# Gated linear attention and top-1 experts on one core: swapped values loaded on their own, masks tied to scalings, the floor inside the scan, copies without gaps

## The chip, the cores and the metric

One core of one Trainium2 chip runs the whole program. The metric is the device time of one execution in microseconds. The kernel before took 412.81 us in the median of three runs (411.1, 412.81 and 415.93).

## The reference

Two stages. The first is an attention without softmax, with a state that decays by channel: B=4, H=8, S=768, D=48, all in fp32, and alpha between 0.8 and 1:

```python
for t in range(S):
    state = alpha[:, :, t, :, None] * state + np.einsum('bhd,bhe->bhde', k[:, :, t], v[:, :, t])
    y[:, :, t] = np.einsum('bhd,bhde->bhe', q[:, :, t], state)
```

The second takes the 3072 rows of 384 (all heads of a token), adds a bias by modality to the logits of eight experts, takes the highest, and computes `gate * (relu(x @ w1[e]) @ w2[e])` with 1024 hidden channels for that expert alone.

## The kernel before

**Tiling of the attention.** 24 units of 128 tokens (`NU`), six to a sequence (`NC`), each with all eight heads as four pairs (`NP`); a head's 48 channels lie in 64 partitions or columns, with a gap of 16. Within a unit the recurrence is solved with scans and matmuls:

- `load` (L148): alpha, k and q of a unit go into one of four sets of buffers (`nat_a0` to `nat_a3`, likewise k and q), v into one of six (`vt0` to `vt5`). Tokens are partitions, and each token brings eight runs of 192 bytes. All are issued on SP's queue.
- `turn_decay` (L247): PE turns alpha, ACT copies it to X (L249).
- `decay`: a scan on DVE from the right gives G, the products of decays up to the unit's end (L258); its floor `amin` by a `tensor_scalar` (L262); a reciprocal of that (L263); a second scan from the left gives Fw (L264).
- `scale_k`, `scale_q`: PE turns k and q, DVE multiplies by G (kh, L280) and Fw (qh, L286).
- `scores`: PE multiplies kh with qh (L301); ACT copies the result to scT in two pieces (L302, L306); POOL clears what lies above the diagonal in two halves with `affine_select` (L305), then copies the values of four heads from one half of the partitions to the other, vt to vs (L309), since half of the products need them there.
- `keys`: PE turns kh back (L317), ACT copies it to knat (L319).
- `combine`: U is the state times the unit's whole decay (L335, DVE); y and the state's update are accumulated by small matmuls (L342); S, the new state, is an addition on DVE.
- `outputs`, `rows`, `logits_turned`, `logits`: ACT copies y to yt (L397); PE turns it (L404), ACT copies it to xs (L409), and SP stores it (L410); the router's logits come from yt by matmuls (L416), in one step out of two for two units.
- `guard` (L268): one ACT instruction that accumulates relu of alpha's bits less a bound over the unit. Its sum tells, after the loop, whether any alpha lay out of range, in which case a slow path computes the attention again.

**Staging.** A step `s` of the loop (L845) works on several units at once: it loads ahead, turns the decays of unit `s`, scales k and q of `s-1`, makes scores and keys of `s-2`, combines `s-3`, and puts out `s-4`. After the loop the expert stage runs, for the most part matmuls.

**What sets the order.** A scheduler places each instruction in its engine's queue from the data's dependences and its own model of times. Every engine works through its own queue in order, and SP's queue issues the loads and stores in order. `issue_after(name)` holds an instruction behind the one marked with that name; `pin` keeps PE's instructions of the loop in program order from the fifth step on. So the queues of ACT, DVE, POOL and SP may come out in another order when an instruction is added or moved elsewhere.

Of the kernel before, what the change touches and what calls it, by code (L numbers as in the profile page):

```python
# [8 lines left out]
F32 = mybir.dt.float32  # L9
# [5 lines left out]
ALU = mybir.AluOpType  # L15
# [6 lines left out]
P = 128  # L22
B, H, S, D = 4, 8, 768, 48
# [31 lines left out]
def attention_moe(ctx: ExitStack, tc: tile.TileContext, q, k, v, alpha, mid, wg, mb, w1, w2, out):  # L55
# [29 lines left out]
    for i in range(NB):  # L85
        for n, val in (("a", 1.0), ("k", 0.0), ("q", 0.0)):
            t = ac.tile([P, H, 64], F32, name=f"nat_{n}{i}")
            nat[n, i] = t
            pool.memset(t[:, :, D:], val)

    VT = []
    for i in range(NV):
        t = ac.tile([P, H, 64], F32, name=f"vt{i}")
        VT.append(t)
        pool.memset(t[:, :, D:], 0.0)
    VS = []
    for i in range(2):
        t = ac.tile([P, NP, 64], F32, name=f"vs{i}")
        VS.append(t)
        pool.memset(t[:, :, D:], 0.0)  # L100
# [12 lines left out]
    def issue_after(name):  # L113
        return tc.issue_after(mark[name].ins) if name else nullcontext()
# [28 lines left out]
    def load(i, names="akqv"):  # L143
        b, c = divmod(i, NC)
        for n, t in (("a", alpha), ("k", k), ("q", q), ("v", v)):
            if n in names:
                src = t[b, :, c * P : (c + 1) * P, :].rearrange("h t d -> t h d")
                sp.dma_start((VT[i % NV] if n == "v" else nat[n, i % NB])[:, :, :D], src)  # L148

    wgs = cp.tile([P, ND, E], F32, name="wgs")  # L150
    sp.dma_start(wgs, wg.rearrange("(c p) e -> p c e", p=P))
# [15 lines left out]


    DR = ac.tile([P, NP * SEG + 1], F32, name="DR")
    vec.memset(DR, 0.0)  # L170
    vec.memset(DR[:, SEG :: SEG], 1.0)
    X, DF, UB = [], [], []
    for i in range(2):
# [64 lines left out]
    def seg(t, lo):  # L238
        return t.rearrange("p (a b) -> p a b", b=SEG)[:, :, lo : lo + P]
# [13 lines left out]
    def decay(i):  # L253
        x, d = X[i % 2], DF[i % 2]
        Fw = sb.tile([P, NP * SEG], F32, name="Fw", bufs=3)
        G = sb.tile([P, NP * SEG + 1], F32, name="G", bufs=4)
        with issue_after("kh" if i else None):
            vec.tensor_tensor_scan(  # L258
                G[:, 1:][:, ::-1], x[:, 1:][:, ::-1], DR[:, 1:][:, ::-1], 0.0, op0=ALU.mult, op1=ALU.add
            )  # L260
        ac1 = amin[:, i]
        vec.tensor_scalar(ac1, G[:, 1::SEG], AFLOOR, None, op0=ALU.max)  # L262
        vec.reciprocal(d[:, 0::SEG], ac1)  # L263
        vec.tensor_tensor_scan(Fw, x[:, :-1], d, 0.0, op0=ALU.mult, op1=ALU.add)  # L264
        st[i, "G"], st[i, "F"] = G, Fw

# [16 lines left out]
    def scale_q(i):  # L283
        qh = sb.tile([P, NP, P], F32, name="qh", bufs=3)
        pq = trans(i, "q")
        vec.tensor_tensor(qh, pq, seg(st[i, "F"], 1), op=ALU.mult)  # L286
        st[i, "q"] = qh

    def scores(i):

        kh, qh = st[i, "k"], st[i, "q"]
        s = sb.tile([P, 12, 64], F32, name="scT")
        pp = banks.rearrange("p g (x t) -> p g x t", t=64)
        for z in range(2):
            for o in range(2):
                for a in range(2):
                    for g in range(2):
                        j, r = 2 * a + o, slice(64 * g, 64 * g + D)
                        x = slice(j, j + 1) if z else slice(j, 4 + o + 1, 4 - 2 * a)
                        t = halves[1] if z else slice(0, P)  # L300
                        pin(pe.matmul(pp[halves[z ^ a], g, x], kh[r, j, halves[z]], qh[r, j, t], start=True, stop=True))  # L301
        act.copy(s[:, :8].rearrange("p (g x) t -> p g x t", g=2), pp[:, :, :4])  # L302
        for b in range(2):
            m = s[halves[b], :8]
            pool.affine_select(m, m, [[0, 8], [1, 64]], ALU.is_ge, 0.0, base=0, channel_multiplier=-1)  # L305
        mark["sc"] = act.copy(s[:, 8:].rearrange("p (g x) t -> p g x t", g=2), pp[:, :, 4:6])  # L306
        st[i, "s"] = s
        for b in range(2):
            mark["vs"] = pool.tensor_copy(VS[i % 2][halves[b], :, :D], VT[i % NV][halves[1 - b], H // 2 :, :D])  # L309

    def keys(i):

        kh = st[i, "k"]
        if i % NC < NC - 1:
            p = ps.tile([P, NP, P], F32, name="tr", bufs=3)
            for j in range(NP):
                pin(pe.transpose(p[:, j], kh[:, j], ident))  # L317
            kn = sb.tile([P, NP, P], F32, name="knat")
            act.copy(kn, p)  # L319
            st[i, "n"] = kn  # L320

    def chain(ins, other, kind):
        info = mybir.DependencyInfo(kind, mybir.DependencyReason.DATA)
        tc.add_manual_dep(ins.ins, other.ins.name, info, reason="row tiles")
        return ins

    def combine(i):

        c = i % NC
        qh, vt, vs, sc = st[i, "q"], VT[i % NV], VS[i % 2], st[i, "s"]  # L330
        U = UB[i % 2]
        if c > 0:
            S0 = st[i, "S"]
            A = st[i, "G"][:, 1::SEG].unsqueeze(2).broadcast_to([P, NP, D])
            vec.tensor_tensor(U[:, :, :D], S0, A, op=ALU.mult)  # L335

        yk = ps.tile([P, 2, 512], F32, name="y")
        fresh = {(b, x) for b in range(2) for x in range(2)}
# [2 lines left out]
        def part(b, x, lo, hi, *operands, stop=False):  # L341
            ins = pin(pe.matmul(yk[halves[x], b, lo:hi], *operands, start=(b, x) in fresh, stop=stop))  # L342
            fresh.discard((b, x))
            if done:
                chain(ins, done[-1], mybir.DependencyClass.NoSync)
            if gate:
                chain(ins, gate.pop(), mybir.DependencyClass.Sync)
            done.append(ins)

        def phase(n):  # L350
            if n:
                gate.append(chain((pool if i < NU - 3 else act).nop(), done[-1], mybir.DependencyClass.Sync))
            if c > 0 and n == 0:
                for a in range(2):
                    for o in range(2):
                        for g in range(2):
                            j = 2 * a + o
                            part(g, o, P * a, P * (a + 1), U[halves[g], j], qh[halves[g], j])
            if c < NC - 1:
                kn = st[i, "n"]  # L360
                for a in range(2):
                    for o in range(2):
                        for g in range(2):
                            j, r, lo = 2 * a + o, halves[o ^ n], 2 * P + D * a
                            part(o, g, lo, lo + D, kn[r, j, halves[g]], vt[r, 2 * j + g, :D])
            for a in range(2):
                for g in (a, 1 - a):
                    for o in range(2):
                        r, z = halves[g ^ n], g ^ n ^ a
                        h = 4 * a + 2 * o + g  # L370
                        xs = (4 * g + 2 * a + o, 8 + 2 * g + o)
                        cuts = ((0,), (1,)) if n and z == 0 and c == 0 else ((0, 1),) if z == 0 else ((0,),)
                        for cut in cuts:
                            x = slice(xs[cut[0]], xs[cut[-1]] + 1, xs[1] - xs[0])
                            lo = P * a + 64 * (z or cut[0])
                            last = n == 1 and a == 1 and cut == cuts[-1]
                            part(g, o, lo, lo + 64 * len(cut), vs[r, h - H // 2] if a else vt[r, h], sc[r, x], stop=last)
# [21 lines left out]

    def rows(i):  # L400

        p = ps.tile([P, NP, P], F32, name="tr", bufs=3)
        for j in range(NP):
            pin(pe.transpose(p[:, j], st[i, "y"][:, j], ident))  # L404
        xs = sb.tile([P, DM], F32, name="xs", bufs=4)
        xv = xs.rearrange("p (a o g d) -> p g a o d", a=2, o=2, g=2)
        pv = p.rearrange("p (g a) (o e) -> p g a o e", g=2, o=2)
        for g in range(2):
            act.copy(xv[:, g], pv[:, g, :, :, :D])  # L409
        sp.dma_start(xd[row(i) : row(i) + P, :], xs)  # L410

    def logits_turned(i):
# [407 lines left out]

    def early(e):
        early_places(e)
        with issue_after("vs"):
            gather(e, row(EARLY[e]))

    def early_gates():
        with issue_after("vs"):
            for e in range(NA):
                gather_gates(e, row(EARLY[e]))

# [14 lines left out]
    for s in range(NU + 3):  # L845
# [4 lines left out]
            turn_decay(s)  # L850
        if 0 <= s - 4:
            outputs(s - 4)
        if s == NU + 1:
            first_inputs()
        if 0 <= s - 1 < NU:
            scale_k(s - 1)
        if 0 <= s - 1 < NU:
            scale_q(s - 1)
        if s < NU:
            decay(s)  # L860
        if s > 4 and s % 2 == 0 and s <= NU:
            logits(s - 5)
        if s > 4 and s % 2:
            logits_turned(s - 4)
        if 0 <= s - 4:
            rows(s - 4)
        if 0 <= s - 2 < NU:
            keys(s - 2)
        steps = combine(s - 3) if 0 <= s - 3 < NU else iter(())
        if s == NU + 2:  # L870
            first_layer(0, 0, own=True)
# [3 lines left out]
        if s == NU + 2:  # L875
            first_layer(0, 1)
        next(steps, None)
        if s < NU:
            guard(s)
        if s == 5:  # L880
# [250 lines left out]
```

## Time and profile before

| | |
|---|---|
| median of the runs | 412.81 us (411.1 to 415.93) |
| profiled execution | 411.67 us, span 409.9 us, clock 0.976 |
| PE busy over the span | 365.8 us (89%) |
| DVE busy | 278.2 us (68%) |
| ACT busy | 214.7 us (52%) |
| POOL busy | 159.2 us (39%) |

The span holds the attention loop with its start-up in the first 172 us or so, and the expert stage behind it. The shares over the whole span hide that the two have different limits, so windows of the timeline are read for the loop: 16 to 40 us (start-up), 40 to 130 us (even steps) and 130 to 172 us (the loop's end). A step of the loop is told by PE's turning of alpha (`tr<-ident,nat_a`, L244): the seventh begins at 39.52 us, the twenty-second at 129.40 us. In a row of the timeline stand the start, the duration, the engine, the line, the operation and its tiles, how many instructions the row holds, and in brackets the idle time before it with what ended it. In a row of a group stand the busy time, the mean of one in ns, and the idle time before with its releasers.

### The profile page before, as it was taken

To read this page: it belongs to the slowest core of one execution; us is meant where nothing else is said; L and a number is where in the kernel's file an instruction comes from. 1 tells how busy PE (TensorE), PEld (TensorE's weight loads), DVE (VectorE), ACT (ScalarE), POOL (GpSimd) and SP (SyncE) were. 2 spreads that over 40 slices of the span, in tenths; PEclk is the share of its full clock that TensorE was granted. 3 is DMA by queue.
4 is the path that set the end of the run, shared out by engine and by line. 5 is a ranking of instruction groups with operands and counts; after the bars stand their busy time and mean duration, and the time that the engine had idled before them with its cause. 6 is when DMAs were issued, how large, how long until landed. Compare 5 with 4: busy or idle time off the path is not lost. (4 is left out here: it accounts for less than half of the span.)

```text
span 409.9 us, 11915 instructions
## 1 busy us (share of the span) xinstructions
PE 365.8 (89%) x4779; PEld 340.4 (83%) x4779; DVE 278.2 (68%) x550; ACT 214.7 (52%) x425; POOL 159.2 (39%) x224
## 2 busy tenths in 40 slices
PE   4867878898989878998997999999999999999993
PEld 3656768777768766778996999999999999999993
DVE  6984978997999993579659394745838465472420
ACT  3445466556566434445458384664837547473430
POOL 8603553454454353501747324233432523221010
PEclk9996999999999988999998999999999999999998
DMA  7999777868876176803998756929656683730000
GB/s 137 189 188 226 167 168 168 163 146 176 169 160 154 42 248 231 297 22 118 387 380 292 267 173 218 302 86 340 219 205 207 208 302 104 295 100 19 21 25 25
DMA packets 132664, 75.26 MB, mean 184 GB/s; under 512 B 103777, under 2 KB 120222, under 8 KB 132600
## 3 DMA queue, kind: packets, MB, share of 16 engines
q1 hardware_dynamic: 128504, 64.57, 56.2%
q0 software_dynamic: 4096, 9.85, 7.0%
q8 instruction: 39, 0.64, 0.6%
q14 instruction: 25, 0.20, 0.1%
HBM read 64.95 MB, written 9.65 MB: 182 GB/s over the span
## 5 line engine op out<-in xcount | busy, mean ns | idle before, releaser
L976 PE MATMUL tr<-xL,w1H 128*128 128x256 f32 x264 | 74.8, 288 | 0.0
L977 PE MATMUL tr<-xH,w1L 128*128 128x256 f32 x264 | 74.0, 285 | 0.0
L975 PE MATMUL tr<-xH,w1H 128*128 128x256 f32 x264 | 72.5, 286 | 1.7 <-DVE hL L982 1.7
L998 PE MATMUL sc<-w2H,hH 128*128 128x384 f32 x192 | 65.8, 343 | 2.3 <-ACT hH L979 1.3
L305 POOL TENSOR_SCALAR_AFFINE_SELECT scT<-scT 64x512 f32<-64x512 f32 x48 | 34.3, 715 | 79.2 <-ACT scT L302 67.2
L999 PE MATMUL sc<-w2L,hH 128*128 128x384 f32 x192 | 64.5, 336 | 0.0
L1000 PE MATMUL sc<-w2H,hL 128*128 128x384 f32 x192 | 64.4, 336 | 0.0
L949 DVE TENSOR_TENSOR w2L<-w2r,w2H 128x768 fp32r<-128x768 f32 x52 | 49.2, 957 | 20.2 <-ACT w2H L947 18.3
L916 POOL DMA_INDIRECT out_dram<-os,odx x25 | 26.7, 1068 | 89.7 <-ACT os L1002 60.9
L949 DVE TENSOR_TENSOR w1L<-w1r,w1H 128x768 fp32r<-128x768 f32 x44 | 41.5, 955 | 22.1 <-ACT w1H L947 22.1
L975 PEld LDWEIGHTS tr<-xH,w1H 128*128 128x128 f32 x264 | 49.9, 193 | 2.1 <-issue 1.9
L947 ACT CAST w2H<-w2r 128x768 fp32r<-128x768 f32 x52 | 42.4, 835 | 16.6 <-PE sc L1000 16.6
L976 PEld LDWEIGHTS tr<-xL,w1H 128*128 128x128 f32 x264 | 51.1, 193 | 0.0
L977 PEld LDWEIGHTS tr<-xH,w1L 128*128 128x128 f32 x264 | 51.0, 193 | 0.0
L725 POOL DMA_INDIRECT xg<-xd,idx x26 | 27.9, 1073 | 55.1 <-PE y L937 46.5
L947 ACT CAST w1H<-w1r 128x768 fp32r<-128x768 f32 x44 | 36.0, 835 | 15.9 <-PE tr L976 15.1
L998 PEld LDWEIGHTS sc<-w2H,hH 128*128 128x128 f32 x192 | 36.1, 188 | 4.3 <-ACT hH L979 1.5
L982 DVE SCALAR_TENSOR_TENSOR hL<-tr,hH 128x512 fp32r<-128x512 f32 x46 | 31.3, 683 | 11.0 <-ACT hH L979 11.0
L268 ACT ACTIVATE junk<-nat_a,bhi 128x384 f32<-128x384 uint32 x24 | 14.8, 617 | 42.8 <-DMA nat_a<-in_alpha_dram 42.7
L258 DVE TENSOR_TENSOR_SCAN G<-X,DR 128x516 f32<-128x516 f32 x24 | 33.3, 1388 | 5.4 <-ACT X L249 5.0
L999 PEld LDWEIGHTS sc<-w2L,hH 128*128 128x128 f32 x192 | 36.2, 188 | 0.0
L1000 PEld LDWEIGHTS sc<-w2H,hL 128*128 128x128 f32 x192 | 36.1, 188 | 0.0
(220 smaller groups left out, 756.7 us busy)
## 6 DMA issues: line engine op xcount, KB each, us to landing
w1r<-in_moe_w_dram SPq DMA_DIRECT2D x26, 768.0 KB, 7.2
w2r<-in_moe_w_dram SPq DMA_DIRECT2D x26, 768.0 KB, 7.5
nat_a<-in_alpha_dram SPq DMA_DIRECT2D x24, 192.0 KB, 3.6
nat_k<-in_k_dram SPq DMA_DIRECT2D x24, 192.0 KB, 3.4
nat_q<-in_q_dram SPq DMA_DIRECT2D x24, 192.0 KB, 3.5
vt<-in_v_dram SPq DMA_DIRECT2D x24, 192.0 KB, 3.5
xd<-xs SPq DMA_DIRECT2D x24, 192.0 KB, 2.9
xg<-xd,idx POOLq DMA_INDIRECT x26, 3.9
```

The source lines that it names most:

```text
L258: vec.tensor_tensor_scan(G[:, 1:][:, ::-1], x[:, 1:][:, ::-1], DR[:, 1:][:, ::-1], 0.0, op0=ALU.mult, op1=ALU.add)
L305: pool.affine_select(m, m, [[0, 8], [1, 64]], ALU.is_ge, 0.0, base=0, channel_multiplier=-1)
L725: pool.indirect_dma_start(xg[i % NX][:, u], None, xd[0:rows], ix, bounds_check=rows - 1, oob_is_err=False)
L947: act.copy(hi, src)
L949: vec.tensor_tensor(lw, src, hi.bitcast(F32), op=ALU.subtract)
L975: pe.matmul(hp[:, z], wH[:, d, fs], xH[:, d], start=(d == 0), stop=False)
L976: pe.matmul(hp[:, z], wH[:, d, fs], xL[:, d], start=False, stop=False)
L977: pe.matmul(hp[:, z], wL[:, d, fs], xH[:, d], start=False, stop=(d == ND - 1))
L982: mark[f"h{j}L"] = vec.scalar_tensor_tensor(hL, hp, 0.0, hH.bitcast(F32), op0=ALU.max, op1=ALU.subtract)
L998: pe.matmul(op, hH[:, z, us], wH[:, z], start=(f == 0), stop=False)
L999: pe.matmul(op, hH[:, z, us], wL[:, z], start=False, stop=False)
L1000: pe.matmul(op, hL[:, z, us], wH[:, z], start=False, stop=(f == NF - 1))
```

## The change

1. **Swapped values.** `vs` is no longer copied by POOL. Behind each load of v, two loads of half the partitions and half the heads bring the other half's values from HBM; `vs` has six buffers instead of two.
2. **Masks.** POOL's two `affine_select` of a unit move one step later, to a function of their own; the first is tied behind U (DVE), the second behind kh (DVE). U is computed earlier in the step, in `state`. The gathers of the expert stage that were held behind the vs copies are now held behind a mask.
3. **Floor.** The scan of G takes the maximum with the floor at each element (`max` with DR in place of adding DR), so the reciprocal reads G. ACT copies the last column of G to `amin`, once a unit; the scan is held behind qh instead of kh.
4. **Copies.** `knat` and `xs` are copied without the gaps of 16, xs in one instruction instead of two, knat into two buffers of its own. `keys` stands ahead of `rows` in the step.

```diff
@@ load
                 sp.dma_start((VT[i % NV] if n == "v" else nat[n, i % NB])[:, :, :D], src)
+                for z in range(2 if n == "v" else 0):
+                    sp.dma_start(VS[i % NV][halves[1 - z], :, :D], src[halves[z], H // 2 :])
@@ set-up
-    vec.memset(DR, 0.0)
+    vec.memset(DR, AFLOOR)
@@ decay
-        with issue_after("kh" if i else None):
+        with issue_after("qh" if i else None):
             vec.tensor_tensor_scan(
-                G[:, 1:][:, ::-1], x[:, 1:][:, ::-1], DR[:, 1:][:, ::-1], 0.0, op0=ALU.mult, op1=ALU.add
+                G[:, 1:][:, ::-1], x[:, 1:][:, ::-1], DR[:, 1:][:, ::-1], 0.0, op0=ALU.mult, op1=ALU.max
             )
-        ac1 = amin[:, i]
-        vec.tensor_scalar(ac1, G[:, 1::SEG], AFLOOR, None, op0=ALU.max)
-        vec.reciprocal(d[:, 0::SEG], ac1)
+        vec.reciprocal(d[:, 0::SEG], G[:, 1::SEG])
@@ scores
-        for b in range(2):
-            m = s[halves[b], :8]
-            pool.affine_select(m, m, [[0, 8], [1, 64]], ALU.is_ge, 0.0, base=0, channel_multiplier=-1)
...
-        for b in range(2):
-            mark["vs"] = pool.tensor_copy(VS[i % 2][halves[b], :, :D], VT[i % NV][halves[1 - b], H // 2 :, :D])
@@ keys
-            act.copy(kn, p)
+            kn = KN[i % 2]
+            act.copy(kn[:, :, :, :D], p[:, :, :, :D])
@@ new functions
+    def state(i):
+        if i % NC:
+            A = st[i, "G"][:, 1::SEG].unsqueeze(2).broadcast_to([P, NP, D])
+            mark["U"] = vec.tensor_tensor(UB[i % 2][:, :, :D], st[i, "S"], A, op=ALU.mult)
+
+    def mask(i):
+        s = st[i, "s"]
+        for b, behind in enumerate(("U", "kh")):
+            m = s[halves[b], :8]
+            ins = pool.affine_select(m, m, [[0, 8], [1, 64]], ALU.is_ge, 0.0, base=0, channel_multiplier=-1)
+            if behind in mark:
+                chain(ins, mark[behind], mybir.DependencyClass.Sync)
+            mark["mask"] = ins
@@ rows
-        for g in range(2):
-            act.copy(xv[:, g], pv[:, g, :, :, :D])
+        act.copy(xs.rearrange("p (x g d) -> p g x d", x=4, g=2), p.rearrange("p (g a) o d -> p g (a o) d", g=2)[:, :, :, :D])
@@ the loop
             turn_decay(s)
         if 0 <= s - 4:
             outputs(s - 4)
+        if 0 <= s - 3 < NU:
+            state(s - 3)
...
             scale_q(s - 1)
+        if 0 <= s - 3 < NU:
+            mask(s - 3)
         if s < NU:
             decay(s)
...
+        if 0 <= s - 2 < NU:
+            keys(s - 2)
         if 0 <= s - 4:
             rows(s - 4)
-        if 0 <= s - 2 < NU:
-            keys(s - 2)
...
+        if 0 < s <= NU:
+            act.copy(amin[:, s - 1], st[s - 1, "G"][:, 1::SEG])
         if s < NU:
             guard(s)
```

The scheduler's queues move with it. First SP's queue around the load of alpha for unit 13 (`nat_a1`, with k and q in `nat_k0` and `nat_q0`, and v of a unit ahead in `vt5`), between two stores of xs. Before:

```order
L410 DMA xd_60<-xs_1011 128x384
L148 DMA vt5_111<-in_v_dram 128x8x48
L148 DMA nat_a1_83<-in_alpha_dram 128x8x48
L148 DMA nat_k0_79<-in_k_dram 128x8x48
L148 DMA nat_q0_81<-in_q_dram 128x8x48
L410 DMA xd_60<-xs_1116 128x384
```

and now:

```order
L417 DMA xd_60<-xs_1029 128x384
L153 DMA vt5_115<-in_v_dram 128x8x48
L155 DMA vs5_127<-in_v_dram 64x4x48 x2
L153 DMA nat_k0_79<-in_k_dram 128x8x48
L153 DMA nat_q0_81<-in_q_dram 128x8x48
L153 DMA nat_a1_83<-in_alpha_dram 128x8x48
L417 DMA xd_60<-xs_1131 128x384
```

The two vs loads stand behind vt, and alpha has moved from second to last. It stands so for units 13, 14, 19, 21 and 23, and between k and q for unit 20; for the others alpha is still ahead of k and q, behind vs.

Next ACT's queue in the same step (`nat_a1` in `guard`; `scT` is the next scores). Before:

```order
L397 COPY yt_980<-y_1023 128x512
L268 ACTIVATE junk_171,gacc_169<-nat_a1_83,bhi_167 128x384
L418 COPY lts_1109<-rt_1104 128x256
L409 COPY xs_1116<-tr_1111 128x4x48 x2
L319 COPY knat_1125<-tr_1120 128x512
L302 COPY scT_1144<-sc_71 128x512
```

and now:

```order
L407 COPY yt_990<-y_1032 128x512
L425 COPY lts_1118<-rt_1113 128x256
L319 COPY knat1_103<-tr_1120 128x8x48
L890 COPY amin_188<-G_1109 128x4
L416 COPY xs_1131<-tr_1126 128x2x4x48
L273 ACTIVATE junk_189,gacc_187<-nat_a1_83,bhi_185 128x384
L307 COPY scT_1151<-sc_71 128x512
```

`guard` has moved from behind yt to just ahead of scT, and the copy of amin is new.

Last, ACT's queue in the start-up, around the X of unit 5 (`X1`), with the guards of units 6, 7 and 8 (`nat_a2`, `nat_a3`, `nat_a0`). Before:

```order
L268 ACTIVATE junk_171,gacc_169<-nat_a2_89,bhi_167 128x384
L302 COPY scT_547<-sc_71 128x512
L306 COPY scT_547<-sc_71 128x256
L268 ACTIVATE junk_171,gacc_169<-nat_a3_95,bhi_167 128x384
L249 COPY X1_161<-tr_596 128x4x128
L397 COPY yt_483<-y_522 128x512
L418 COPY lts_628<-rt_623 128x256
L268 ACTIVATE junk_171,gacc_169<-nat_a0_77,bhi_167 128x384
```

and now:

```order
L273 ACTIVATE junk_189,gacc_187<-nat_a2_89,bhi_185 128x384
L307 COPY scT_563<-sc_71 128x512
L308 COPY scT_563<-sc_71 128x256
L273 ACTIVATE junk_189,gacc_187<-nat_a3_95,bhi_185 128x384
L273 ACTIVATE junk_189,gacc_187<-nat_a0_77,bhi_185 128x384
L256 COPY X1_179<-tr_611 128x4x128
L407 COPY yt_500<-y_538 128x512
```

The guard of unit 8 now stands ahead of X and yt; before, it came behind both.

More of the change, by code (lines that the diff above doesn't have):

```diff
@@ L89, in attention_moe @@
             pool.memset(t[:, :, D:], val)
+    KN = []
+    for i in range(2):
+        t = ac.tile([P, NP, 2, 64], F32, name=f"knat{i}")
+        KN.append(t)
+        pool.memset(t[:, :, :, D:], 0.0)
     VT = []
@@ L96, in attention_moe @@
     VS = []
-    for i in range(2):
+    for i in range(NV):
         t = ac.tile([P, NP, 64], F32, name=f"vs{i}")
@@ L285, in scale_q @@
         pq = trans(i, "q")
-        vec.tensor_tensor(qh, pq, seg(st[i, "F"], 1), op=ALU.mult)
+        mark["qh"] = vec.tensor_tensor(qh, pq, seg(st[i, "F"], 1), op=ALU.mult)
         st[i, "q"] = qh
@@ L314, in keys @@
         if i % NC < NC - 1:
-            p = ps.tile([P, NP, P], F32, name="tr", bufs=3)
+            p = ps.tile([P, NP, 2, 64], F32, name="tr", bufs=3)
             for j in range(NP):
                 pin(pe.transpose(p[:, j], kh[:, j], ident))
-            kn = sb.tile([P, NP, P], F32, name="knat")
-            act.copy(kn, p)
+            kn = KN[i % 2]
+            act.copy(kn[:, :, :, :D], p[:, :, :, :D])
             st[i, "n"] = kn
@@ L325, in chain @@
         return ins
+    def state(i):
[10 more added lines that the diff above has]
+            mark["mask"] = ins
     def combine(i):
         c = i % NC
-        qh, vt, vs, sc = st[i, "q"], VT[i % NV], VS[i % 2], st[i, "s"]
+        qh, vt, vs, sc = st[i, "q"], VT[i % NV], VS[i % NV], st[i, "s"]
         U = UB[i % 2]
[L332 to L335, printed above, removed]
         yk = ps.tile([P, 2, 512], F32, name="y")
@@ L364, in phase @@
                             j, r, lo = 2 * a + o, halves[o ^ n], 2 * P + D * a
-                            part(o, g, lo, lo + D, kn[r, j, halves[g]], vt[r, 2 * j + g, :D])
+                            part(o, g, lo, lo + D, kn[r, j, g], vt[r, 2 * j + g, :D])
             for a in range(2):
@@ L400, in rows @@
     def rows(i):
-        p = ps.tile([P, NP, P], F32, name="tr", bufs=3)
+        p = ps.tile([P, NP, 2, 64], F32, name="tr", bufs=3)
         for j in range(NP):
@@ L405, in rows @@
         xs = sb.tile([P, DM], F32, name="xs", bufs=4)
-        xv = xs.rearrange("p (a o g d) -> p g a o d", a=2, o=2, g=2)
-        pv = p.rearrange("p (g a) (o e) -> p g a o e", g=2, o=2)
-        for g in range(2):
-            act.copy(xv[:, g], pv[:, g, :, :, :D])
+        act.copy(xs.rearrange("p (x g d) -> p g x d", x=4, g=2), p.rearrange("p (g a) o d -> p g (a o) d", g=2)[:, :, :, :D])
         sp.dma_start(xd[row(i) : row(i) + P, :], xs)
@@ L822, in early @@
         early_places(e)
-        with issue_after("vs"):
+        with issue_after("mask"):
             gather(e, row(EARLY[e]))
     def early_gates():
-        with issue_after("vs"):
+        with issue_after("mask"):
             for e in range(NA):
```

## The prediction

> **What bounds the kernel now.** I read the busy shares by stage first. The three windows are the start-up, the even middle of the attention loop and its tail. After the window's length the columns are busy time and instruction counts, the granted TensorE clock, the DMA share and GB/s:
>
> ```profile
> core 0: us, PE busy (x) PEld busy (x) DVE busy (x) ACT busy (x) POOL busy (x), PEclk, DMA share, GB/s
> 16.00:40.00 24.00, 18.13 (x380) 15.10 (x381) 15.95 (x26) 11.49 (x30) 6.82 (x10) 0.86 0.99 200
> 40.00:130.00 90.00, 78.14 (x1947) 67.13 (x1945) 80.64 (x163) 52.63 (x141) 43.43 (x61) 1.00 0.78 169
> 130.00:172.00 42.00, 35.05 (x781) 29.38 (x780) 29.76 (x110) 17.34 (x43) 18.65 (x29) 0.92 0.59 198
> ```
>
> The start-up is bound by transfers (0.99). In the middle no engine is full: DVE idles 9.4 of 90 us, PE 11.9, ACT 37.4. Something passes between them, so the waits come next (us in total, times, longest):
>
> ```profile
> ACT junk L268 <- DMA nat_a<-in_alpha_dram: 42.7, 22, 3.3
> PEld rt L416 <- ACT yt L397: 13.5, 10, 4.4
> DVE G L258 <- ACT X L249: 5.0, 5, 3.4
> ```
>
> ACT, the least busy engine of the three, stands 42.7 us in `guard` (L268) for alpha to land; the copies queued behind it (scT, X, yt) then hold PE (13.5) and DVE (5.0). One step of the timeline shows the loop; these are ACT's, SP's and PE's rows:
>
> ```profile
> 88.45 0.54 ACT L409 COPY xs<-tr 128x192 f32<-128x192 f32 x2
> ...
> 93.85 0.61 ACT L268 ACTIVATE junk<-nat_a,bhi 128x384 f32<-128x384 uint32 x1 [3.13 <-DMA nat_a<-in_alpha_dram]
> ...
> 94.47 0.52 ACT L409 COPY xs<-tr 128x192 f32<-128x192 f32 x2
> 94.88 0.60 ACT L319 COPY knat<-tr 128x512 f32<-128x512 f32 x1
> 95.35 0.61 ACT L302 COPY scT<-sc 128x512 f32<-128x512 f32 x1
> ...
> 96.09 0.63 ACT L249 COPY X<-tr 128x512 f32<-128x512 f32 x1
> 96.57 0.64 ACT L397 COPY yt<-y 128x512 f32<-128x512 f32 x1
> ```
>
> ```profile
> 89.02 0.36 SPq L410 DMA_DIRECT2D xd<-xs  x1
> 89.48 0.51 SPq L148 DMA_DIRECT2D vt<-in_v_dram  x1
> 90.08 0.63 SPq L148 DMA_DIRECT2D nat_a<-in_alpha_dram  x1
> 90.80 0.58 SPq L148 DMA_DIRECT2D nat_k<-in_k_dram  x1
> ```
>
> ```profile
> 39.52 0.66 PE L244 MATMUL tr<-ident,nat_a 128*128 128x128 f32 x4
> ...
> 93.74 0.66 PE L244 MATMUL tr<-ident,nat_a 128*128 128x128 f32 x4
> ...
> 97.26 0.64 PE L416 MATMUL rt<-yt,wgp 128*32 128x256 f32 x8 [1.07 <-ACT yt L397]
> ...
> 100.92 0.66 PE L244 MATMUL tr<-ident,nat_a 128*128 128x128 f32 x4
> ...
> 106.17 0.66 PE L244 MATMUL tr<-ident,nat_a 128*128 128x128 f32 x4
> ...
> 129.40 0.66 PE L244 MATMUL tr<-ident,nat_a 128*128 128x128 f32 x4
> ```
>
> Read it as a ring. ACT's xs copy ends at 88.99; SP stores it, issues vt at 89.48 and alpha at 90.08; `guard` starts at 93.85, 4.4 us after vt's issue; five copies follow, yt ends at 97.21, PE takes the logits, and the next step begins at 100.92, 3.7 after yt's end. The xs copy at 94.47, itself behind that guard, sends the next load. Fifteen steps lie between 39.52 and 129.40: 89.88 us, 5.99 each.
>
> To test the ring I wrote it as a recurrence: vt is issued 0.49 after xs ends or at the step's start T, whichever is later; alpha lands 4.45 later; ACT runs its queue in order with the gaps above (guard 0.62, xs 0.41, knat 0.47, scT pair 0.74, X 0.48, yt 0.64); T comes 3.95 after yt ends in odd steps (logits ahead) and 3.4 in even ones, close to the 3.7 and, from the next step, 3.5 of the trace. It gives 87.6 us for the fifteen steps against 89.88 measured, with DVE nowhere in it.
>
> **Part 1: values swapped by their own loads.** Two half-width loads per unit stand on SP between vt and alpha; together they carry half of one load. The start-up prices a load where DMA is full:
>
> ```profile
> 17.15 0.62 ACT L268 ACTIVATE junk<-nat_a,bhi 128x384 f32<-128x384 uint32 x1 [1.83 <-DMA nat_a<-in_alpha_dram]
> ...
> 31.31 0.62 ACT L268 ACTIVATE junk<-nat_a,bhi 128x384 f32<-128x384 uint32 x1
> ...
> 31.92 0.58 ACT L249 COPY X<-tr 128x512 f32<-128x512 f32 x1
> ...
> 34.77 0.62 ACT L268 ACTIVATE junk<-nat_a,bhi 128x384 f32<-128x384 uint32 x1 [0.21 <-DMA nat_a<-in_alpha_dram]
> ```
>
> The first of these waits for the 13th load issued, the last (unit 8) for the 30th: 17.62 us for 17 loads, 1.04 each, so 0.52 a pair by data. By issue, two at 0.36 to 0.51 (the xd and vt rows) are 0.7 to 1.0. Alpha lands 0.5 to 0.9 later; I take 0.65. With 5.1 for 4.45 the recurrence on the old queues gives 93.6: **+5.9**. POOL is rid of the vs copies; their 30.8 us were not on the ring:
>
> ```profile
> L309 POOL COPY vs<-vt 64x192 f32<-64x192 f32 x48 | 30.8, 642 | 7.9 <-PE y L342 3.7 <-DMA vt<-in_v_dram 1.7
> ```
>
> **Part 2: the order that comes with it.** SP now issues alpha behind k and q for units 13, 14, 19, 21 and 23, behind k for unit 20. Alpha then lands after two more loads, 2.1 us by the 1.04 (from 1.3 by the issues of alpha and k, 0.63 and 0.58). ACT's queue puts `guard` last before scT in most of these. The recurrence with the new SP and ACT orders, 5.1 and 2.1, and T 2.9 after yt in even steps (part 4), gives 100.5: **+12.9** with part 1; with 1.3 and 4.95 it falls to +9, with 5.4 it rises to +16. I take **+11**, toward the low end, because alpha's extra delay is part queue and not all data at a DMA share of 0.78.
>
> In the start-up ACT's old order has unit 7's guard ahead of X (31.92); the new one has unit 8's too. That is the 30th load with seven pairs ahead: 34.77 + 7 x 0.52 = 38.4, a guard, X at 39.0 instead of 31.92: 7.1 later. Before, 7.6 us pass from that X to the step at 39.52, with transfers still short; some waits behind the later X will have been served meanwhile, so 5.2 to 7.2 reach the loop: **+6**. The lower end is the length of a step with nothing to wait for (106.17 - 100.92 = 5.25, in place of 7.6).
>
> The Trainium skill, "DMA: Bandwidth & Descriptors", section Specifications, asks for 512 B per transfer for line rate, and below that tells of a read-modify-write; this load has runs of 192 B. The 200 GB/s at a share of 0.99 agrees. By that rule the pair costs by its count of runs, half a load's, which is also the 0.52.
>
> **Part 3: masks and scans.** Beside POOL's mask DVE's G scan is long, beside its copy it is not:
>
> ```profile
> 65.19 1.37 POOL L305 TENSOR_SCALAR_AFFINE_SELECT scT<-scT 64x512 f32<-64x512 f32 x2 [3.56 <-ACT scT L302]
> ...
> 70.81 1.52 POOL L305 TENSOR_SCALAR_AFFINE_SELECT scT<-scT 64x512 f32<-64x512 f32 x2 [2.62 <-ACT scT L302]
> 72.39 1.70 POOL L309 COPY vs<-vt 64x192 f32<-64x192 f32 x2
> ```
>
> ```profile
> 65.92 1.73 DVE L258 TENSOR_TENSOR_SCAN G<-X,DR 128x516 f32<-128x516 f32 x1 [0.15 <-ACT X L249]
> ...
> 72.33 1.22 DVE L258 TENSOR_TENSOR_SCAN G<-X,DR 128x516 f32<-128x516 f32 x1
> ```
>
> ```profile
> L258 DVE TENSOR_TENSOR_SCAN G<-X,DR 128x516 f32<-128x516 f32 x24 | 33.3, 1388 | 5.4 <-ACT X L249 5.0
> ...
> L280 DVE TENSOR_TENSOR kh<-tr,G 128x512 f32<-128x512 f32 x24 | 16.4, 685 | 3.5 <-PE tr L244 3.4
> ...
> L335 DVE TENSOR_TENSOR UB<-S,G 128x192 f32<-128x192 f32 x20 | 9.2, 458 | 0.4
> ...
> L262 DVE TENSOR_SCALAR amin<-G 128x4 f32<-128x4 f32 x24 | 3.8, 160 | 0.0
> ```
>
> Moved beside U, kh and qh, the masks free 33.3 - 24 x 1.22 = 4.0 us of G scans; the amin row gives 3.8 more. U, already 0.458 on average, may get longer: tied to it stands half a mask. So DVE loses 0.3 a step. None of it shortens the ring, which has no DVE in it: 0, with -0.3 x 15 = -5 as the bound if DVE paces some steps. The amin copy on ACT costs 0.19 a step (the amin row's 0.16 and a little more), already in the 100.5. The scan's floor is one instruction with another operation: 0. The new wait: POOL's second mask behind kh; queued behind it is the next unit's work and gathers, and PE's y matmuls wait. In the step from 93.74 logits start at 97.26 and the y matmuls come behind, so 3.5 after T or later; k's turning is over at T + 1.3 (two groups of 0.66), kh takes 0.69 and the mask 0.7 (1.37 for two): 2.7. The cover is 0.8; gone, a mask's 0.7 a step shows.
>
> The Trainium skill, "GPSIMD Engine Reference", Key points, says POOL shares its SBUF interfaces with VectorE and contends with instructions of two SBUF inputs. By that rule every overlap of a scan with POOL costs, copies too, and the saving would be the whole excess. The trace agrees for the mask (1.73) and not for the copy at 72.39 (1.22), so the excess of 4.0 measured is the most there is.
>
> **Part 4: copies without gaps, keys ahead of rows.** xs is one copy for two, knat 384 elements for 512:
>
> ```profile
> L409 ACT COPY xs<-tr 128x192 f32<-128x192 f32 x48 | 12.8, 319 | 8.6 <-PE tr L404 8.6
> ...
> L319 ACT COPY knat<-tr 128x512 f32<-128x512 f32 x20 | 11.8, 588 | 3.7 <-PE tr L317 3.7
> ```
>
> That is at most 0.1 a step on ACT. With keys' four transposes in front, one group fewer stands behind yt: about 0.5 in even steps, which is the 2.9 above. After the loop's last loads the tail (three steps from 129.40) keeps this and the lighter DVE: 3 x 0.5 = **-1.5** (-3 to +1).
>
> **Sum**, against the profiled execution's 411.67 us (span 409.9, and 1.8 around it; 0.3% under the median of 412.81): 411.7 + 6 + 11 - 1.5 = **427**. The expert stage is as before and starts that much later.
>
> **The rivals.** *Faster: DVE paces the middle.* It is busy 80.64 of 90, and 85.6 with its waits for X. Then a step falls by what DVE sheds: 4.0 + 3.8 over 24 steps, 0.33, and the 0.33 of waits for X (5.0 over 15) go too, together 0.65 x 15 = 10 us, within PE's 11.9 idle. Start-up 0, for its DMAs are 0.99 full either way and the order is ACT's: 411.7 - 10 = **402**. Against it: with DVE pacing, ACT could not make PE wait 13.5 for yt, and the recurrence without DVE lands within 3%. It decides if alpha lands before ACT reaches `guard`.
>
> *No change: later loads, but hidden.* With `guard` later in ACT's queue its wait shrinks by what alpha is late, and start-up's +6 is offset by the tail and 5 of DVE: 411.7 + 6 - 1.5 - 5 = **411**. For it: DMA's share of 0.78 leaves room; with the old loads the new ACT queue costs only 1.2 in the recurrence (88.8). Against: in the loop alpha is late relative to its own xs, which moves along.
>
> *The masks wait.* The cover of 0.8 goes and the second mask shows, 0.7 x 15 = 10 on top: **437**. It needs kh to be late by 0.8 in each step; before, kh waits 3.5 over all 24 (its row above).
>
> **How the numbers follow.** My ring gets 0.62, hidden loads 0.13, DVE 0.2, masks 0.05. The ring's own range is 411.7 + 5 + 9 - 3 = 423, less 5 if DVE paces some steps, 418, to 411.7 + 7 + 16 + 1 = 436. To leave out no more than 0.2, the range takes in the hidden case and reaches 404, the slower part of DVE's. A measurement of this kernel tells 1%, about 4 us, from no change. Faster by over 1%: 0.2. Within: the hidden case, 0.13. Slower: 0.67.
>
> **What would show it.** ACT's wait in `guard` for alpha stays 40 us or more and the median step in the middle is 6.5 to 6.8 us with DVE busier nowhere; X of unit 5 is near 39; alpha lands 5 us or more after vt's issue, 7 where k and q go first; G scans at 1.22. I am wrong if PE's waits for yt vanish and steps fall to 5.4 or so (DVE paced them), or if alpha lands within 4.5 us of vt in spite of the pair.

## The result, and the profile after

The changed kernel takes 446.66 us in the median (446.07 to 453.74) against 412.5 us of the kernel before: 1.0805 times as long, 95% interval 1.0737 to 1.0874. In a later session on the chip it took 1.0995 times as long (1.0871 to 1.1118). Forecast were 427 us, 404 to 437: the side was right, but of the 34 us only 15 were forecast, and the time lies above the range.

The first profiled execution of the changed kernel was a disturbed one (453.74 us), so the rows below come from a second profile of the same code, and stand beside a second profile of the kernel before. The two were taken in different sessions, in which the kernel before had medians of 416.12 and 413.03 us; 3 us of their difference belong to that, and the tail is what differs most between sessions, as the experiments show.

I cut both executions at the same four points: PE's turning of alpha for the first, the seventh and the twenty-second unit, the first matmul with w2, and the last. The kernel before, then the changed kernel; columns are the window, its length, busy time of each engine, granted TensorE clock, DMA share, GB/s:

```profile
4.52:39.88 35.36, 26.25 (x457) 21.65 (x457) 25.79 (x43) 16.68 (x41) 16.15 (x37) 0.90 0.95 189
39.88:130.89 91.01, 78.65 (x1947) 66.93 (x1943) 79.89 (x162) 52.43 (x140) 44.51 (x60) 1.00 0.79 168
130.89:183.75 52.86, 45.69 (x851) 38.14 (x846) 38.34 (x135) 24.43 (x58) 20.38 (x30) 0.94 0.50 168
183.75:404.90 221.15, 216.97 (x1533) 215.02 (x1533) 131.55 (x202) 120.24 (x187) 74.03 (x68) 0.98 0.59 199
```

```profile
4.50:51.39 46.89, 28.35 (x457) 23.95 (x457) 24.60 (x37) 18.41 (x48) 11.47 (x35) 0.75 0.85 171
51.39:159.45 108.06, 84.55 (x1949) 71.24 (x1944) 76.36 (x146) 51.24 (x138) 19.63 (x30) 0.94 0.71 149
159.45:222.44 62.99, 50.17 (x849) 40.98 (x845) 36.83 (x133) 23.95 (x54) 16.69 (x20) 0.86 0.43 144
222.44:446.32 223.88, 218.14 (x1532) 215.17 (x1533) 131.42 (x202) 120.03 (x187) 73.69 (x68) 0.98 0.58 196
```

The start-up is 11.5 us longer, the fifteen middle steps 17.1, the tail 10.1, the expert stage 2.7. In the first profiles of both kernels (411.67 and 453.74 us) the same four differences are 10.4, 24.2, 5.8 and 1.5 us. What the change took from its engines is there: POOL is busy 19.6 us in the middle for 44.5, DVE 76.4 for 79.9. Yet the DMA share falls everywhere, and the array runs at less than full clock in the middle (0.94), which it did not before. Everything waits more.

The waits of the changed kernel name the same place as before, larger (42.7 us there, 13.5 for yt, 5.0 for X), and a new one, PE for a mask:

```profile
ACT junk L273 <- DMA nat_a<-in_alpha_dram: 60.6, 20, 6.3
...
PEld rt L423 <- ACT yt L407: 22.7, 10, 11.9
...
PEld y L352 <- POOL scT L336: 5.4, 3, 4.4
```

SP's queue of the changed kernel around unit 13 shows where alpha went:

```profile
73.74 0.40 SPq L153 DMA_DIRECT2D vt<-in_v_dram  x1
74.23 1.84 SPq L155 DMA_DIRECT2D vs<-in_v_dram  x2
76.17 0.56 SPq L153 DMA_DIRECT2D nat_k<-in_k_dram  x1
76.81 0.53 SPq L153 DMA_DIRECT2D nat_q<-in_q_dram  x1
77.40 0.85 SPq L153 DMA_DIRECT2D nat_a<-in_alpha_dram  x1
```

Alpha is issued 3.66 us after vt; in the step quoted before it was 0.60. The two vs loads alone hold the queue 1.84 us; a pair takes 1.36 us in the median, and 3.26 at most. For units 9 to 23 alpha is issued 0.67 us behind vt in the median before and 3.02 us now, while `guard` starts 3.7 us after alpha's issue before and 3.6 now. So what alpha lost in the middle, it lost in SP's queue and not on its way. Over the whole run one vs load, with a quarter of vt's data, takes longer to issue than vt (minimum, median, maximum in ns):

```profile
L153 SPq DMA_DIRECT2D vt<-in_v_dram x24: 368/386/1211, 7.4 to 159.9; - x24
```

```profile
L155 SPq DMA_DIRECT2D vs<-in_v_dram x48: 595/616/2602, 10.4 to 161.1; - x48
```

### The profile page after: what moved, and what is told of

It reads as the page before. It is cut to its first block, busy times and chain, and to the rows that moved or that the text cites. A ratio compares the mean times of both kernels' runs of the same rounds, so it can differ in the third digit from the quotient of the medians.

```text
span 452.0 us, 11904 instructions
## 1 busy us (share of the span) xinstructions
PE 380.3 (84%) x4779; PEld 352.4 (78%) x4779; DVE 272.0 (60%) x526; ACT 215.0 (48%) x425; POOL 126.9 (28%) x182
## 5 line engine op out<-in xcount | busy, mean ns | idle before, releaser
L336 POOL TENSOR_SCALAR_AFFINE_SELECT scT<-scT 64x512 f32<-64x512 f32 x48 | 32.2, 670 | 153.9 <-ACT scT L307 82.0
```

The source lines that it names most:

```text
L336: ins = pool.affine_select(m, m, [[0, 8], [1, 64]], ALU.is_ge, 0.0, base=0, channel_multiplier=-1)
```

## The experiments

All ratios are to the kernel before in the same session, with 95% intervals. The theory after the result: a ring through ACT's `guard` (alpha's load, guard, the copies behind it, yt, PE's next step, xs, the next load), into which the vs loads put time on SP. The rivals: the masks' waits, the extra work on ACT, or the transfers themselves.

**Part 1 alone.** The kernel before, with

```diff
+                for z in range(2 if n == "v" else 0):
+                    sp.dma_start(VS[i % NV][halves[1 - z], :, :D], src[halves[z], H // 2 :])
...
-            mark["vs"] = pool.tensor_copy(VS[i % 2][halves[b], :, :D], VT[i % NV][halves[1 - b], H // 2 :, :D])
```

> The kernel before with part 1 alone: the vs loads in place of POOL's copies, masks, scans and copies as before. Ring theory (the pair of vs loads holds SP's queue 1.3 to 3.3 us in the trace of after, alpha lands later, ACT's guard waits, everything behind it waits): most of the 34 us, so 432 to 448 us, and the wait of guard for alpha above 50 us. Rival (parts 2 to 4 make the loss: masks tied behind U and kh, the extra copy on ACT): 408 to 416 us.

(`vs` has six buffers here too, and the gathers are held behind the second mask.) Measured: 1.0917 (1.084 to 1.0995), a median of 456.39 us beside 417.72, and guard's wait 59.9 us. That is above the 432 to 448 us expected, in a session in which the kernel before was 5 us slower too. Part 1 by itself gives the whole loss; its middle, 118.8 us, is even longer than the changed kernel's.

**All but part 1.**

```diff
-                for z in range(2 if n == "v" else 0):
-                    sp.dma_start(VS[i % NV][halves[1 - z], :, :D], src[halves[z], H // 2 :])
...
+        for b in range(2):
+            mark["vs"] = pool.tensor_copy(VS[i % 2][halves[b], :, :D], VT[i % NV][halves[1 - b], H // 2 :, :D])
```

> The changed kernel with part 1 undone: POOL copies vt to vs again (in two buffers, behind the scores), parts 2 to 4 stay. Ring theory: guard's wait is back near 43 us or less, and the lighter DVE and the shorter row behind yt may show: 398 to 413 us. Rival (the masks or ACT's order make the loss): 430 us or more.

Measured: 1.0213 (1.0144 to 1.0281), guard's wait 40.4 us. Neither theory: most of the loss is gone, as the ring says, but 2% stay where I had expected a gain. Its middle is 92.5 us, about as before (39.16 to 131.69); its tail is 65.4 us, for 59.7 of a kernel with the masks in their old place in the same session (the late guard, below). The cause stands in POOL's rows and PE's row:

```profile
153.84 1.24 POOL L732 DMA_INDIRECT xg<-xd,idx  x1 [1.29 <-issue]
155.39 1.01 POOL L732 DMA_INDIRECT xg<-xd,idx  x1 [0.30 <-issue]
156.46 0.65 POOL L336 TENSOR_SCALAR_AFFINE_SELECT scT<-scT 64x512 f32<-64x512 f32 x1
161.93 0.66 POOL L336 TENSOR_SCALAR_AFFINE_SELECT scT<-scT 64x512 f32<-64x512 f32 x1 [4.82 <-DMA xg<-xd,idx]
```

```profile
162.64 0.37 PE L352 MATMUL y<-scT,vt 64*64 64x64 f32 x2 [5.04 <-POOL scT L336]
```

The gathers of the expert stage go out just ahead of a unit's masks, and the second mask starts only when the gathered rows have landed; kh, to which it is tied, was done at 155.0. The kernel before has the same wait, but only 0.68 us of it, since its mask has to wait for its scores until then; masks moved a step later are due while the gathers are still on their way. Why this mask waits for a gather at all is not shown.

**The late guard.** Both kernels with guard behind yt's copy, so that the alpha it reads landed steps ago:

```diff
+            mark["X"] = mark["late"] = turned
...
+        with issue_after("late" if i else None):
             act.activation(junk..., nat["a", i % NB]..., AF.Relu, bias=bhi, accum_out=gacc[:, i : i + 1])
...
-            act.copy(yt[:, i % 2]...
+            mark["late"] = act.copy(yt[:, i % 2]...
```

> The kernel before with one edit: guard is held behind yt's copy of its own unit (X in the first units), so the alpha that it reads landed steps ago. Ring theory: guard's wait for alpha goes from 42.7 us to almost nothing; the middle steps fall from 5.99 to what DVE's work gives, 80.64 / 15 = 5.4, so 9 us less, and 3 to 6 us less in the start-up, 397 to 404 us. Rival (the wait in guard is idle time that costs nothing, DVE or transfers pace the loop): 409 to 416 us.

> The kernel before with the late guard again, in five rounds beside the one above: 0.96 to 0.975 of the kernel before by the first measurement of 0.966.

Measured for the kernel before with it: 0.9662 (0.958 to 0.9744), and 0.971 (0.9666 to 0.9753) in another session; guard's wait is out of the list. Its middle (second session) is 84.4 us for 91.0, and the start-up 31.5 for 35.4:

```profile
4.50:36.01 31.51, 26.55 (x457) 22.59 (x457) 25.64 (x43) 15.23 (x36) 15.72 (x38) 0.84 0.91 178
36.01:120.44 84.43, 78.14 (x1947) 67.21 (x1943) 79.03 (x160) 54.75 (x140) 41.32 (x60) 1.00 0.90 194
```

That execution took 405.14 us, above its kernel's median of 401.7, but its middle ran at full clock (1.00). The ring did set the pace of the kernel before. With it gone, a step is 5.63 us (5.4 was expected), and PE (78.1 of 84.4) and DVE (79.0) are both nearly full.

> The changed kernel with the same edit: guard behind yt. Ring theory: the vs loads are still there, but nothing on ACT waits for alpha any more; alpha is needed four steps after its load; 392 to 404 us, below the kernel before. Rival (the loads cost by the bandwidth they take, or the masks by their waits): 430 us or more.

Measured: 1.0028 (0.9984 to 1.0071). That falls between: guard gives back most of the 8%, and the middle is 84.8 us (39.06 to 123.89), as with POOL's copies, in spite of loads, masks and amin. What is left, against the kernel before with the late guard in the same session, lies in the start-up (PE's seventh step at 39.06 for 33.64) and in the tail (63.9 us for 59.7), where PE waits 6.6 us for masks.

**The changed kernel again**, whose profile is shown above.

> The changed kernel once more, as it is, for a profile beside those of the experiments: 8% over the kernel before, guard's wait for alpha 55 to 60 us, and PE waiting 5 us once for a mask behind the gathers.

Measured: 1.0995 (1.0871 to 1.1118); guard's wait 60.6 us, and PE once 4.1 us for a mask.

**Alpha first on SP.** The same loads, v and vs held behind alpha's. To get there, v and its pair are also loaded two steps later than in the changed kernel:

```diff
+                with issue_after("la" if n != "a" and "la" in mark else None):
...
-            load(s + PF - 1)
+            load(s + PF - 1, "akq")
+        if 3 <= s < NU:
+            load(s, "v")
```

> The changed kernel with the loads of v and vs held behind alpha's on SP (v of unit s is loaded in step s, behind alpha of unit s + 2): the same loads, but alpha is always the first of a step. Theory that the queue's order makes the loss (the vs pair's time on SP and alpha behind k and q): guard's wait falls to 45 us or less and the time to 1.01 to 1.035 of the kernel before, which leaves the masks' 2%. Rival (the pair costs by what it takes of the transfers, wherever it stands): 1.06 or more.

Measured: 1.0392 (1.0323 to 1.0461), a little over the 1.01 to 1.035 expected; guard's wait 44.3 us, as in the kernel before, and the middle is 88.7 us, a little under the 91.0 of before, at a DMA share of 0.87:

```profile
4.40:48.39 43.99, 28.54 (x457) 23.71 (x457) 24.72 (x37) 18.02 (x48) 11.60 (x36) 0.77 0.88 172
48.39:137.13 88.74, 77.79 (x1949) 66.94 (x1944) 76.02 (x146) 51.06 (x138) 19.68 (x30) 1.00 0.87 182
137.13:199.08 61.95, 47.89 (x850) 39.35 (x846) 36.35 (x133) 23.69 (x54) 16.65 (x20) 0.89 0.46 153
```

So in the middle it was the place in SP's queue, and not the transfers: all loads are made, and nothing is lost. Most of the start-up's loss stays (PE's seventh step at 48.39 for 51.39), and so does the tail's.

**Parts 3 and 4 alone**, with POOL's copies and masks in their old places, and the same with the late guard.

> The changed kernel with parts 1 and 2 undone: POOL copies vt to vs and masks right behind the scores again, U in combine, gathers behind the vs copies; the floor in the scan and the gap-free copies with keys ahead of rows stay. Parts 1, 3 and 4 without the masks were not tried apart; with part 1 undone alone 1.021 of the kernel before was measured. Theory of the masks (their new place puts one of them behind the gathers' landing, so PE waits 5 us and its clock falls): the 2% are gone, 0.98 to 1.00 of the kernel before. Rival (parts 3 and 4 cost it, by ACT's extra copy of amin or by the new order of keys and rows): 1.015 or more.

Measured: 1.0055 (1.0011 to 1.01), just above the 0.98 to 1.00 expected: most of the 2% is the masks', and the floor in the scan and the copies without gaps are worth nothing that shows.

> The kernel with parts 3 and 4 alone, and guard held behind yt. Ring theory: 0.95 to 0.965 of the kernel before, a little under the 0.966 of the kernel before with the late guard, since the loop is then nearer to DVE's work, which the floor in the scan cuts by the amin row's 0.16 us a step. If parts 3 and 4 are worth nothing: 0.966.

Measured: 0.9878 (0.9792 to 0.9965), more than expected, and more than the 0.966 and 0.971 of the plain kernel with the late guard. Its middle is 83.7 us (35.48 to 119.15), below the 84.2 of the plain kernel with the late guard in such a session, its tail 59.9 us for 59.7, and its start-up 31.1 for 29.2. The two profiled executions took 410.17 and 410.59 us, and the second is well above its kernel's faster ones (402 to 408), so the profiles can't give the reason for the 2% between the ratios, and it is not settled.

**Only the last masks back.** Part 1 undone, and the masks of the last four units right behind their scores, without ties:

```diff
+        if i >= TAIL:
+            masks(i, (None, None))
...
     def mask(i):
+        if i < TAIL:
+            masks(i, ("U", "kh"))
```

> The changed kernel with part 1 undone, and the masks of the last four units right behind their scores again; for the other twenty they stay tied behind U and kh. Theory of the masks (only the one behind the gathers' landing costs, once, 5 us and the clock): 1.00 to 1.01 of the kernel before, against 1.021 with all masks moved, and no wait of PE for a mask over 1 us. Rival (the ties cost in every step): 1.02.

Measured: 0.9956 (0.9923 to 0.9989), for 1.0213 with all masks moved; the tail is 53.6 us for 65.4, of which some 5 us are the session's (below). PE waits for no mask longer than 0.3 us; POOL's second mask still waits for gathered rows, but 0.67 us and at a time when its scores have just come:

```profile
152.21 1.24 POOL L741 DMA_INDIRECT xg<-xd,idx  x1 [0.18 <-POOL vs L312]
153.75 1.02 POOL L741 DMA_INDIRECT xg<-xd,idx  x1 [0.30 <-issue]
158.22 0.65 POOL L345 TENSOR_SCALAR_AFFINE_SELECT scT<-scT 64x512 f32<-64x512 f32 x1 [3.45 <-ACT scT L305]
159.54 0.66 POOL L345 TENSOR_SCALAR_AFFINE_SELECT scT<-scT 64x512 f32<-64x512 f32 x1 [0.67 <-DMA xg<-xd,idx]
```

> The kernel before once more, for a profile from the same chip as the experiments: its step pattern as known (T of the twenty-second step near 129), and a stretch from there to the first matmul of w2 between 53 us (then all others lose there) and 60 us (then only the kernels with moved masks do).

Measured in the same session: 413.03 us (1.0018, 0.9976 to 1.0059) and a tail of 52.9 us. In the sessions in which the kernel before took 416 to 418 us, every kernel's tail was near 58 us or more, the one with the late guard alone too (59.7 there, 54.75 here); so tails are compared within a session.

> The same kernel with guard held behind yt. If moved masks, floor and copies are worth something once guard is out of the way: 0.950 to 0.965 of the kernel before. If not: as the kernel before with the late guard, 0.966 to 0.975.

Measured: 0.9675 (0.9625 to 0.9725), a median of 400.01 us against 412.99. That is the lowest median here; beside it the plain kernel with the late guard has 0.971 (0.9666 to 0.9753), which the intervals don't tell apart. So the moved masks, the floor and the copies show no gain of their own.

```profile
4.52:35.02 30.50, 24.13 (x456) 20.41 (x456) 25.21 (x37) 15.67 (x40) 15.12 (x39) 0.94 0.95 184
35.02:118.71 83.69, 76.53 (x1948) 67.35 (x1944) 75.55 (x144) 53.95 (x140) 31.93 (x60) 1.00 0.90 193
118.71:172.36 53.65, 44.32 (x850) 36.45 (x846) 37.68 (x135) 25.58 (x60) 20.48 (x30) 0.97 0.49 168
```

**The changed kernel with the last masks back**, and nothing else.

> The changed kernel with one edit: the masks of its last four units right behind their scores again; the vs loads and guard stay as changed. If the masks alone make the loss behind the attention's middle: the stretch from the twenty-second step to the first matmul of w2 falls from 63 us to 53 to 55, and the time from 1.08 to 1.10 of the kernel before to 1.055 to 1.075. If the vs loads lengthen that stretch by themselves: it stays at 60 us or more.

Measured: 1.0805 (1.0746 to 1.0863); its tail is 58.2 us for 63.0 (155.22 to 213.46), in a session where the kernel before took 417.65 us. That is more than the 1.055 to 1.075 expected, but PE waits for no mask longer than 0.4 us, and the masks make about 5 us of the tail. The 10 us of the table above mix sessions: in those in which the kernel before took 416 to 418 us, kernels with neither vs loads nor moved masks have tails of 59.7 to 60.1 us, so the changed kernel's 63.0 is 3 over them. With part 1 alone and the masks in place the tail is 62.1. So the parts don't add up, and what the loads cost in the tail stays open.

**All three losses away, the loads kept**: last masks back, alpha first, guard late.

> The changed kernel with its three losses taken away and its vs loads kept: the last four masks back, alpha first on SP, guard behind yt. If the loads cost only by what they hold up: 0.965 to 0.975 of the kernel before, as with POOL's copies in the same place (0.9675). If they cost by the transfers themselves: 0.98 or more, with the loss in the start-up, where the transfers are full.

Measured: 1.0172 (1.0096 to 1.0248), against 0.9675 with POOL's copies in the loads' place. The loads still cost: PE's seventh step comes at 38.30 us for 35.02, and the middle takes 88.65 us for 83.69, where PE now waits for alpha's landing itself (5.4 of these 14.0 us in the middle):

```profile
PE tr L254 <- DMA nat_a<-in_alpha_dram: 14.0, 9, 4.3
```

With POOL's copies that wait is 6.0 us, twice, at the start. But the loads alone don't make it: the changed kernel with only the late guard makes the same loads, has a middle of 84.8 us and is the faster of the two (1.0028). So putting alpha first, which helped the ring, costs once guard is late. In both kernels with the loads alpha is issued 3 to 10 us ahead of its step in the middle, mostly under 6; with POOL's copies (the kernel above) it is 9 to 21. So the loads leave little to spare. Whether SP's queue or the transfers use it up is not shown: SP issues for 80.3 of the 88.7 us and for 74.8 of 84.8 with only the late guard, but with POOL's copies and the late guard for 52.6 to 74.5 in four profiles with middles of 83.7 to 84.4; and the DMA share is lower where the middle is slower (0.83, against 0.88 with only the late guard and 0.90 with POOL's copies).

## Why the prediction was right and wrong

The step that failed is the price of the vs pair on SP's queue: 0.65 us in the middle and 0.52 in the start-up were taken, and 1.3 to 1.4 us in the middle and 1.26 in the start-up were measured. The path that it takes, through SP's queue, `guard` and the copies behind it, was right. A second, smaller step failed in the tail: the masks' cover, which gathers ahead of a mask took away.

- **What bounds the kernel: right.** The ring through guard was shown from both ends. Taking guard off it makes the kernel before 2.9 to 3.4% faster; putting alpha first takes the middle of the changed kernel from 108.1 to 88.7 us. The signs named for it came: guard's wait is 60.6 us, the middle step 7.0 in the median (6.5 to 6.8 were named), and guard starts 6.2 us after vt's issue in the median (4.5 before), 6.9 to 8.1 where k and q go first.
- **Part 1, the pair's price: the term that was mis-sized.** I had 0.52 us by its share of the data and 0.7 to 1.0 by two issues of vt's length, and took 0.65. Two issues of 616 ns with the gaps are 1.3 us, and the median pair takes 1.36. A transfer with a quarter of the runs does not issue in a quarter of the time. By the recurrence's own slope (+12.9 us at 0.65, +16 at 0.95) 1.35 us extrapolate to about +20 for the middle, where I had rounded down to +11. Measured were 17.1 and 24.2 in two profiles of the changed kernel, and the middle with only the last masks moved back was 102.9 us, 11.9 over the 91.0 of before. So the price explains the size within a scatter that nothing here explains.
- **Start-up, +6: mis-sized by the same price.** X of unit 5 was forecast at 39.0 us and came at 44.32, behind the two guards that the order showed ahead of it:

```profile
42.96 0.61 ACT L273 ACTIVATE junk<-nat_a,bhi 128x384 f32<-128x384 uint32 x1 [3.67 <-DMA nat_a<-in_alpha_dram]
43.70 0.61 ACT L273 ACTIVATE junk<-nat_a,bhi 128x384 f32<-128x384 uint32 x1
44.32 0.56 ACT L256 COPY X<-tr 128x512 f32<-128x512 f32 x1
```

  Alpha of unit 8, the 30th load without the pairs in both kernels, is the only row of the kernel before, and the second of the changed kernel's two, which begins at 40.41:

```profile
31.57 0.65 SPq L148 DMA_DIRECT2D nat_a<-in_alpha_dram  x1
```

```profile
39.74 1.18 SPq L153 DMA_DIRECT2D nat_a<-in_alpha_dram  x2
```

  That is 8.84 us for the seven pairs ahead of it, 1.26 a pair. In the prediction's own sum 34.77 + 8.8 + 0.6 gives 44.2. I had taken the stage as bound by data (DMA share 0.99). But SP issues almost without a pause in both kernels, 42 times in 35.4 us before and 59 times in 46.9 now, 0.84 and 0.79 us each, while the DMA share falls from 0.95 to 0.85. So in the changed kernel SP's queue is nearer the bound than the transfers; which of the two holds up the other is not shown. With guard late the same pairs leave PE's seventh step at 39.06, 5.4 us behind the 33.64 of the kernel before with the late guard in that session (36.01 in the other); so half or more of the 11.5 us goes through guard, and the rest is the loads' own.
- **Masks, "the cover is 0.8": wrong, in one place.** I named the gathers as queued behind the mask, and looked at kh as what it waits for. What decided was the other side: a mask queued behind the gathers. In the middle the ties cost nothing (84.8 us with them, 84.4 without, guard late). In the tail PE waits 4 to 6 us once. The -1.5 for the tail became +3 to +6 where like sessions are compared, and with all masks moved but no vs loads the tail is 5.6 us over that of the kernel before with the late guard.
- **Scans: the saving did not come.** 33.0 us for 33.3 in the profiles, where I had 4.0 less. The ties hold only a mask's start; the second one, behind kh, runs on into the G scan. U, which I feared would get longer, got shorter (370 ns for 458). Since DVE was not on the ring, nothing hung on either:

```profile
L265 DVE TENSOR_TENSOR_SCAN G<-X,DR 128x516 f32<-128x516 f32 x24 | 33.0, 1376 | 12.1 <-ACT X L256 12.0
...
L330 DVE TENSOR_TENSOR UB<-S,G 128x192 f32<-128x192 f32 x20 | 7.4, 370 | 0.4
```

- **The copy beside the scan: misread.** I took the copy at 72.39 as untouched, because the scan kept its 1.22 us. It was the copy that waited; the last section has the rows.
- **The rival "DVE paces the middle": wrong for the change, near for what comes next.** With guard late DVE is busy 79.0 of 84.4 us. That its 402 us are about what the late guard gives (401.7 in the median) is luck: it counted on a lighter DVE, and the late guard leaves DVE's work as it is.
- **The rival "hidden loads": wrong, since guard's wait rose.** With guard late the loads do hide in the middle (84.8 us for 84.2 in the same session), but not in the start-up.

## What to carry to other kernels

An engine that is busy half the time can pace a loop by one wait in its queue: look at what stands behind the instruction that waits for a transfer, and whether it could read data that landed earlier. Moving work from an idle engine to a queue that feeds the loop is not free because the bytes are few; price it by that queue's issue time, read from loads that stand in the same place. And where an instruction is moved later, look at what stands ahead of it in its new place (here a gather whose landing it has to wait for), as well as at what it was tied to.

## What the hardware showed that I had not expected

**POOL's masks and copies and DVE's scan do not share, one waits for the other.** In the kernel before both cases stand. In the step at 65.19 that the prediction quotes, the second mask began at 65.91 and the scan at 65.92, and the scan grew from 1.22 to 1.73 us. In the step below the second mask began at 55.81 and the scan at 55.82; here the scan kept its 1.23 and the pair of masks grew from 1.37 to 2.41. So where both begin within 0.01 us, either can go first:

```profile
55.10 2.41 POOL L305 TENSOR_SCALAR_AFFINE_SELECT scT<-scT 64x512 f32<-64x512 f32 x2 [3.40 <-ACT scT L302]
```

```profile
55.82 1.23 DVE L258 TENSOR_TENSOR_SCAN G<-X,DR 128x516 f32<-128x516 f32 x1 [0.50 <-ACT X L249]
```

In the changed kernel the scan's excess goes with the overlap: 0.07 us at 0.21, 0.25 at 0.39, 0.50 at 0.65. The Trainium skill, "Trainium Architecture — The Big Picture", section "What this means for kernel authors", says that the port pair of DVE and GpSimd is held by an exclusive lock and not shared by bandwidth; these rows agree. The copies do the same. In the kernel before a copy takes 355 ns in the median, and a pair 0.74 us where no scan runs; the first copy of the pair at 72.39 began 0.06 us behind the scan's start at 72.33 and took 1.30 us, to just past the scan's end at 73.55:

```profile
43.23 0.74 POOL L309 COPY vs<-vt 64x192 f32<-64x192 f32 x2
```

```profile
L309 POOL COPY vs<-vt x48: 339/355/1300, 12.0 to 160.0; 64x192 f32<-64x192 f32 x48
```

**A quarter of the data does not issue in a quarter of the time, and the place in the queue counts.** A vs load takes 616 ns to issue against 386 of vt in the medians. But vt stands right behind the store of xs there. In the run with alpha first vt comes behind alpha, and its median is 691 ns, while alpha's falls from 557 to 450:

```profile
L154 SPq DMA_DIRECT2D nat_a<-in_alpha_dram x24: 368/450/1839, 1.3 to 127.9; - x24
L154 SPq DMA_DIRECT2D vt<-in_v_dram x24: 385/691/2215, 7.0 to 138.8; - x24
```

So 616 against 386 compares two places as well as two loads. What the load's 64 partitions and its strides add was not tried.
